# Seven half-block products in two more groups of layer one, and their input sums made at the end of attention

## The chip, the cores and the metric

The program runs on one core of one Trainium2 chip. The metric is device time in microseconds (us): the median of three runs. One further execution was taken by the hardware profiler, and its trace gives the rows below. Engines are named as the profile names them: PE (matmul), PEld (weight load), DVE (vector), ACT (scalar), POOL (GpSimd), SP (the queue that issues most DMAs).

## The reference, cut to what matters

```python
def _attn_ref(q, k, v):                      # 2 batches, 8 heads, 768 tokens, 64 wide
    k_sum = k.reshape(B, H, nb, block, D).max(axis=3)
    v_sum = v.reshape(B, H, nb, block, D).mean(axis=3)
    scores_l = scale * np.matmul(q, k.transpose(0, 1, 3, 2))      # kept where |i - j| < 16
    scores_s = scale * np.einsum('bhsd,bhnd->bhsn', q, k_sum) + np.log(block)
    ...                                      # softmax over both together
    return np.matmul(a, v_all)

def _moe_ref(x, w_in, w_out):                # 1536 tokens, 512 -> 2048 -> 512
    h = x @ w_in
    g = h * (1.0 / (1.0 + np.exp(-1.702 * h)))
    return g @ w_out

def _moe2_ref(x, w_gate, w_val, w_out):      # 512 -> 1536 (twice) -> 512
    gate = 1.0 / (1.0 + np.exp(-(x @ w_gate)))
    return gate * (x @ w_val) @ w_out
```

The attention's output is the input of layer one (`_moe_ref`), whose output is the input of layer two (`_moe2_ref`).

## The kernel before, in words

**Numbers in two parts.** Each operand of a layer's products is held as a high and a low half (`xH`/`xL`, `w..H`/`w..L`, `gh`/`gl`), and each product is three matmuls of 128x128 weights by 512 columns: high by low, low by high, high by high. A weight arrives as 64-bit words in `raw`. `load` turns it into the halves: DVE takes `da` (L125) and `db` (L128) from the words, ACT scales `da` (L126), DVE joins them (L132), ACT casts the high half (L135), DVE subtracts for the low half (L137).

**Tiles.** There are three blocks of 512 tokens (0, 1, 2). Layer one's hidden width of 2048 is cut into eight groups of 256 columns (`g` 0 to 7), layer two's 1536 into six. For each group and block, `first` makes two hidden tiles (24 matmuls, `ps_h`); ACT takes the sigmoid, DVE multiplies (`sg`, L399), ACT casts `gh` (L400), POOL subtracts for `gl` (L401). Then `second` multiplies by the group's rows of `w_out` (24 matmuls, four tiles `ps_o`), which DVE adds to `acc` (L464); of group 0, ACT copies them (L460).

**Paired groups.** From group `PAIRED` on, blocks 0 and 1 are not computed one by one: `pair` makes a 2x2 product of half blocks with seven products of six matmuls (`product`) in place of eight. For that it needs sums of quarters of the weight (`ws`, L151, then a cast and a subtraction into `s..H` and `s..L`, L158 and L160) and four sums of halves of the blocks 0 and 1 (`input_sums`: whole values `f1` to `f3`, split into `t1`, `t2`, `t3`, and a fourth that overwrites block 1's own tile). Block 2 goes through `single`.

**Order.** Attention has 24 units (batch, group of tokens, pair of heads). A loop over `t` issues each unit's steps with lags: scores `ps_s`, exponentials, the transposition `ps_p` (L633), its copy `pt` out of PSUM (L638, on DVE from unit 10 on), the product with v `ps_x` (L652), then the halves of x: ACT's cast `xH` (L670) and DVE's subtraction `xL` (L673). The `filler` issues layer one's groups 0 and 1 for blocks 0 and 1 in between. After attention come the `steps`: `first` of block 2 for groups 0 and 1, then groups 2 and 3 block by block, each step's `second` after the next step's `first`; then the paired groups. `pull` and `folding` issue pieces of weight loading and of the input sums between them. On top of that, a scheduler at build time chooses the order on each engine by what it expects of each instruction; DVE instructions marked `keep_in_program_order` keep their order among themselves. Each engine runs its own queue in order. The places for weights (`w_a` 8, `w_b` 6, of which `w_b` exists only after attention), the PSUM tiles and the tiles of `tp` are handed on when their last reader is done.

Of the kernel before, what the change touches and what calls it, by code (L numbers as in the profile page):

```python
# [9 lines left out]
F32 = mybir.dt.float32  # L10
F32R = mybir.dt.float32r
# [3 lines left out]
ALU = mybir.AluOpType  # L15
AX = mybir.AxisListType
PSUM = bass.MemoryType.PSUM
P = 128
# [11 lines left out]
def attention_moe_moe2_kernel(ctx: ExitStack, tc: tile.TileContext, ins: dict, out: bass.AP):  # L30
    nc = tc.nc
# [17 lines left out]
    TB = 512  # L49
# [55 lines left out]
    pool([sg_slots], 2, "sg_a")  # L105
    acc_a = ctx.enter_context(tc.tile_pool(name="acc_a", bufs=1))
    ps_h = ctx.enter_context(tc.tile_pool(name="ps_h", bufs=2, space=PSUM))

    def load(layer, g, i, early):

        while len(w_free) < 2:
            yield
        raw, shape = raws.pop(0)
        n = raw.shape[1] // 2
        words = raw.rearrange("p (n t) -> p n t", t=2)
        tail, head = words[:, :, 0], words[:, :, 1]
        a, b = (wtmp.tile([P, n], U32, tag=f"d{x}", name=f"d{x}") for x in "ab")
        af = a.bitcast(F32)  # L120
        ts = nc.vector.tensor_scalar
        hi, lo = (take(list(shape), f"w{layer}_{g}_{i}{x}", (layer, g, i)) for x in "HL")
        flat = "p a n -> p (a n)"

        ts(out=af, in0=head.bitcast(F32), scalar1=F64_MAX, scalar2=-F64_MAX, op0=ALU.min, op1=ALU.max)  # L125
        nc.scalar.activation(af, af, AF.Prelu, scale=REBIAS, alpha=-2.0 ** 32)  # L126
        yield
        ts(out=b, in0=tail, scalar1=29, scalar2=None, op0=ALU.logical_shift_right)  # L128
        if not early:
            fetch()  # L130
        yield
        nc.vector.scalar_tensor_tensor(  # L132
            out=a, in0=a, scalar=3, in1=b, op0=ALU.logical_shift_left, op1=ALU.bitwise_or
        )
        nc.scalar.copy(hi.rearrange(flat), af)  # L135
        yield
        nc.vector.tensor_tensor(out=lo.rearrange(flat), in0=af, in1=hi.rearrange(flat), op=ALU.subtract)  # L137
        weights[layer, g, i] = hi, lo
        yield
        if layer == 1 and (g < PAIRED or i == 1) or layer == 2 and i == 2:  # L140
            yield
            return
        w = af.rearrange("p (a n) -> p a n", n=shape[2])
        s = wtmp.tile([P, 4, KC // 2, P], F32, tag="db", name=f"ws{layer}_{g}_{i}")
        for n, x, y, op in (
            (0, block(w, 1, 0), block(w, 1, 1), ALU.add),
            (1, s[:, 0], block(w, 0, 0), ALU.subtract),
            (2, block(w, 0, 0), block(w, 1, 0), ALU.subtract),
            (3, block(w, 0, 1), s[:, 1], ALU.subtract),
        ):  # L150
            nc.vector.tensor_tensor(out=s[:, n], in0=x, in1=y, op=op)  # L151
            if n == 1:
                yield
        while len(w_free) < 2:
            yield
        sh, sl = (take([P, 4, KC // 2, P], f"s{layer}_{g}_{i}{x}", (layer, g, i, "s")) for x in "HL")
        flat = "p a k f -> p (a k f)"
        nc.scalar.copy(sh.rearrange(flat), s.rearrange(flat))  # L158
        yield
        nc.vector.tensor_tensor(out=sl.rearrange(flat), in0=s.rearrange(flat), in1=sh.rearrange(flat), op=ALU.subtract)  # L160
        weights[layer, g, i, "s"] = sh, sl
        yield
# [28 lines left out]

    mats = {1: [w_in, w_out], 2: [w_gate, w_val, w_out2]}
    pieces, weights, raws = [], {}, []
    PAIRED = 4
    wanted = [(1, g, i) for g in range(n1) for i in range(2)] + [(2, 0, 0), (2, 0, 1)]
    for g in range(n2):
        wanted += [(2, g + 1, 0)] * (g + 1 < n2) + [(2, g, 2)] + [(2, g + 1, 1)] * (g + 1 < n2)
# [20 lines left out]
        return t[:, (LO, HI)[j], i * P:(i + 1) * P]  # L218

    def t_tile(name):  # L220
        return tp.tile([P, KC // 2, TB], F32R, tag=f"t{name}", name=f"t{name}")

    def input_sums():

        def tt(**x):
            tc.keep_in_program_order(nc.vector.tensor_tensor(**x))

        f1, f2, f3 = (tp.tile([P, KC // 2, TB], F32, name=f"f{n}") for n in "123")  # L230
        h1, l1, h3, l3 = (t_tile(x) for x in ("1H", "1L", "3H", "3L"))

        def whole(to, blk, half):
            tt(out=to, in0=xH[blk][:, half], in1=xL[blk][:, half], op=ALU.add)

        whole(f1, 0, LO)
        yield
        whole(f3, 1, LO)
        yield
        tt(out=f1, in0=f3, in1=f1, op=ALU.subtract)  # L240
        yield
        whole(f2, 1, HI)
        yield
        tt(out=f3, in0=f2, in1=f3, op=ALU.subtract)
        nc.scalar.copy(h3, f3)
        yield
        tt(out=f2, in0=f2, in1=f1, op=ALU.subtract)
        nc.scalar.copy(h1, f1)
        yield
        nc.gpsimd.tensor_tensor(out=l3, in0=f3, in1=h3, op=ALU.subtract)  # L250
        yield
        nc.gpsimd.tensor_tensor(out=l1, in0=f1, in1=h1, op=ALU.subtract)
        yield
        h2, l2 = t_tile("2H"), t_tile("2L")
        h4, l4 = xH[1][:, LO], xL[1][:, LO]
        whole(f3, 0, HI)
        yield
        tt(out=f3, in0=f3, in1=f2, op=ALU.subtract)
        nc.scalar.copy(h4, f3)
        nc.scalar.copy(h2, f2)  # L260
        yield
        nc.gpsimd.tensor_tensor(out=l4, in0=f3, in1=h4, op=ALU.subtract)
        yield
        nc.gpsimd.tensor_tensor(out=l2, in0=f2, in1=h2, op=ALU.subtract)
        tsum.update({"1": (h1, l1), "2": (h2, l2), "3": (h3, l3), "4": (h4, l4)})
        yield

    def token_sums():

# [226 lines left out]
    with tc.manual_schedule(engines={mybir.EngineType.SP}), ExitStack() as es:  # L496
# [236 lines left out]
        def filler():  # L733
            for layer, g, blk in steps[:EARLY]:
                while (blk + 1) * 2 * HP - 1 + LD > now[0]:
                    yield
                need((1, g, 0))
                yield from first(layer, g, blk, batch=True)
                need((1, g, 1))
                yield from second(layer, g, blk, False, True)  # L740

        now = [0]
        fill = filler()
        for t in range(-1, NU + LD):
            now[0] = t

# [34 lines left out]
                pull(1 if t < 6 or t > 9 else 2)  # L781
            for _ in range(2 if t >= 8 else 1):
                next(fill, None)
        for _ in fill:
            pull(2)

    with tc.manual_schedule(engines={mybir.EngineType.SP}):
# [7 lines left out]
            for x, n in (("a", 4), ("b", 2))  # L795
        )
        ps_f, ps_s = Slots("h", (ps_a, 4)), Slots("h", (ps_h, 2), (ps_b, 2))
        folding, sums_1 = iter(()), input_sums()

        def run(main, rest=iter(()), after=()):  # L800

# [15 lines left out]
        for step in steps:  # L817
            need((*step[:2], 0))
            run(first(*step))
            if step[2] == 2:  # L820
                drop(*step[:2], 0)
            if prev:
                need((*prev[:2], 1))
                run(second(*prev, False))
                if prev[2] == 2:
                    drop(*prev[:2], 1)
            if step == (1, 2, 0):
                folding = itertools.islice(sums_1, 8)
            elif step == (1, PAIRED - 1, 1):
                for _ in folding:  # L830
                    pass
                folding = sums_1
            prev = step
        top = n1 - 1
        for g in range(PAIRED, n1):
# [94 lines left out]
```

## Time and profile before

| | before |
|---|---|
| three runs | 622.29, 622.41, 623.23 us; median 622.41 us |
| profiled execution | 623.11 us, its span 621.3 us |
| PE busy | 605.5 us, 97% of the span, 3138 instructions |
| DVE busy | 446.5 us, 72% |
| ACT busy | 297.0 us, 48% |
| POOL busy | 207.7 us, 33% |
| granted clock of PE | 1.00 throughout |

The span is the time from the first to the last instruction that the profile shows; the execution is 1.8 us longer. "Busy" of PE counts overlapping matmuls once, so a share of 97% says that PE had something under way, not that it ran at its peak.

### The profile page before, as it was taken

How to read it: one execution, taken by the hardware profiler on the slowest of the kernel's cores; microseconds unless marked ns; L12 is line 12 of the kernel's file. 1: busy time of each engine (PE TensorE's matmuls, PEld its weight loads, DVE VectorE, ACT ScalarE, POOL GpSimd, SP SyncE). 2: the span in 40 equal slices, each digit the busy share in tenths (PEclk: the TensorE clock that was granted, in tenths of full speed). 3: DMA queues.
4: the chain of work that ended last, by engine and by line, in shares of the span. 5: the costliest groups of instructions: out<-in, count | busy, mean ns of one | idle time of the engine just before them, and what ended most of it. 6: DMA issues, size and time to landing. Idle time of an engine off the chain costs nothing.

```text
span 621.3 us, 8331 instructions
## 1 busy us (share of the span) xinstructions
PE 605.5 (97%) x3138; PEld 493.4 (79%) x3138; DVE 446.5 (72%) x652; ACT 297.0 (48%) x580; POOL 207.7 (33%) x168
## 2 busy tenths in 40 slices
PE   7698999999999999999999999999999999999997
PEld 4576787788878888888888888888888888888886
DVE  6699666489998877887679996268488587493424
ACT  4688657565434353435346555454244353252210
POOL 6796685223453323223322031221220221120210
PEclk9999999999999999999999999999999999999999
DMA  9998743044121213031001214023024023000004
GB/s 307 339 311 295 233 134 70 0 137 136 68 69 68 69 24 112 25 112 64 5 18 51 68 69 136 1 69 129 7 68 136 0 74 131 0 2 0 1 34 170
DMA packets 25160, 58.08 MB, mean 93 GB/s; under 512 B 1568, under 2 KB 1824, under 8 KB 25120
## 3 DMA queue, kind: packets, MB, share of 16 engines
q1 hardware_dynamic: 24400, 56.24, 27.9%
q10 hardware_dynamic: 720, 1.31, 0.6%
q8 instruction: 25, 0.41, 0.3%
q14 instruction: 15, 0.12, 0.1%
HBM read 53.08 MB, written 3.15 MB: 90 GB/s over the span
## 4 chain that ended last, share of the span: by engine, by line
PE 81%; DMA 8%; DVE 5%; POOL 3%; issue 2%; ACT 1%; SPq 0%; POOLq 0%; ACTq 0%
PE ps_o L384 33%; PE ps_v L173 12%; PE ps_y L173 11%; PE ps_h L173 9%; PE ps_x L173 7%; PE ps_h L384 5%; DMA xH<-in_moe_w_out 3%; DMA k<-in_k 3%; DMA vt<-in_vt 2%; PE ps_s L600 2%; POOL gl L401 1%; PE ps_x L652 1%; PE ps_p L633 1%; DVE da L132 1%; DVE w_0L L137 1%
## 5 line engine op out<-in xcount | busy, mean ns | idle before, releaser
L401 POOL TENSOR_TENSOR gl<-sg,gh 128x512 fp32r<-128x512 f32 x84 | 121.9, 1455 | 364.6 <-ACT gh L400 309.6
L464 DVE TENSOR_TENSOR acc<-ps_o,acc 128x512 f32<-128x512 f32 x143 | 96.0, 684 | 56.7 <-PE ps_o L384 56.7
L400 ACT CAST gh<-sg 128x512 fp32r<-128x512 f32 x84 | 51.7, 620 | 67.7 <-DVE sg L399 47.3
L384 PE MATMUL ps_o<-gl,w_1H 128*128 128x512 f32 x192 | 75.5, 394 | 0.7 <-POOL gl L401 0.7
L384 PE MATMUL ps_o<-gh,w_1H 128*128 128x512 f32 x192 | 74.7, 390 | 0.0
L384 PE MATMUL ps_o<-gh,w_1L 128*128 128x512 f32 x192 | 72.1, 396 | 1.5 <-ACT gh L400 1.4
L384 PE MATMUL ps_o<-w_2H,gh 128*128 128x512 f32 (+1 forms) x146 | 56.4, 386 | 0.0
L384 PE MATMUL ps_o<-w_2L,gh 128*128 128x512 f32 (+1 forms) x146 | 56.4, 386 | 0.0
L384 PE MATMUL ps_o<-w_2H,gl 128*128 128x512 f32 (+1 forms) x146 | 55.9, 387 | 0.1
L132 DVE SCALAR_TENSOR_TENSOR da<-da,db 128x1024 uint32<-128x1024 uint32 x34 | 45.4, 1334 | 8.2 <-ACT da L126 7.6
L126 ACT ACTIVATE da<-da 128x1024 f32<-128x1024 f32 x34 | 36.0, 1060 | 19.9 <-DVE da L125 17.5
L384 PEld LDWEIGHTS ps_o<-gh,w_1L 128*128 128x128 f32 x192 | 35.9, 188 | 9.4 <-ACT gh L400 2.0
L384 PEld LDWEIGHTS ps_o<-gl,w_1H 128*128 128x128 f32 x192 | 36.1, 188 | 8.9 <-POOL gl L401 1.9
L384 PEld LDWEIGHTS ps_o<-gh,w_1H 128*128 128x128 f32 x192 | 36.1, 188 | 7.2
L589 POOL TENSOR_SCALAR kx<-k 128x384 f32<-128x384 f32 x24 | 32.4, 1351 | 20.2 <-DMA k<-in_k 11.2
L613 ACT ACTIVATE e<-ps_s,nm 128x128 f32<-128x128 f32 x96 | 34.3, 381 | 9.3 <-DVE nm L605 8.2
L384 PE MATMUL ps_h<-xL,w_0H 128*128 128x512 f32 x96 | 37.6, 392 | 0.4 <-DVE xL L673 0.4
L384 PE MATMUL ps_h<-xH,w_0L 128*128 128x512 f32 x96 | 37.7, 401 | 0.0
L384 PE MATMUL ps_h<-xH,w_0H 128*128 128x512 f32 x96 | 37.4, 390 | 0.0
L384 PEld LDWEIGHTS ps_o<-w_2H,gl 128*128 128x128 f32 x146 | 27.4, 188 | 6.1 <-DVE acc L464 0.3
L399 DVE TENSOR_TENSOR sg<-ps_h,sg 128x512 f32<-128x512 f32 x32 | 21.8, 684 | 14.3 <-ACT sg L408 12.2
L384 PEld LDWEIGHTS ps_o<-w_2H,gh 128*128 128x128 f32 x146 | 27.4, 188 | 5.6
(223 smaller groups left out, 1410.1 us busy)
## 6 DMA issues: line engine op xcount, KB each, us to landing
raw<-in_moe_w_out SPq DMA_DIRECT2D x13, 1024.0 KB, 4.9
raw<-in_moe_w_in SPq DMA_DIRECT2D x8, 1024.0 KB, 7.5
raw<-in_moe_w_gate SPq DMA_DIRECT2D x6, 1024.0 KB, 5.0
raw<-in_moe_w_val SPq DMA_DIRECT2D x6, 1024.0 KB, 5.1
q<-in_q SPq DMA_DIRECT2D x20, 256.0 KB, 9.5
vwin<-in_v SPq DMA_DIRECT2D x6, 768.0 KB, 9.7
k<-in_k SPq DMA_DIRECT2D x8, 400.0 KB, 7.6
out<-acc SPq DMA_DIRECT2D x11, 256.0 KB, 2.0
```

What stands on the lines that cost most here:

```text
L126: nc.scalar.activation(af, af, AF.Prelu, scale=REBIAS, alpha=-2.0 ** 32)
L132: nc.vector.scalar_tensor_tensor(out=a, in0=a, scalar=3, in1=b, op0=ALU.logical_shift_left, op1=ALU.bitwise_or)
L137: nc.vector.tensor_tensor(out=lo.rearrange(flat), in0=af, in1=hi.rearrange(flat), op=ALU.subtract)
L173: nc.tensor.matmul(ps, lhsT=a[x][:, kk, :], rhs=b[y][:, kk, :], start=start and i == 0, stop=i == n - 1, skip_group_check=True,)
L384: nc.tensor.matmul(ps, lhsT=a, rhs=b, start=i == 0, stop=i == n - 1)
L399: nc.vector.tensor_tensor(out=sg, in0=val, in1=sg, op=ALU.mult)
L400: nc.scalar.copy(gh, sg)
L401: nc.gpsimd.tensor_tensor(out=gl, in0=sg, in1=gh, op=ALU.subtract)
L464: nc.vector.tensor_tensor(out=a[:, m, :], in0=ps, in1=a[:, m, :], op=ALU.add)
L589: nc.gpsimd.tensor_scalar(out=to, in0=x, scalar1=scale, scalar2=None, op0=ALU.mult)
L600: nc.tensor.matmul(ps[:, j, :], lhsT=t[:, j, :], rhs=kt[:, j, :], start=False, stop=j == G - 1)
L613: nc.scalar.activation(e[:, j, :], s[:, j, :], AF.Exp, bias=nm[:, j:j + 1], accum_out=sm[:, j:j + 1])
```

## The change

`PAIRED` goes from 4 to 2: groups 2 and 3 of layer one go through `pair` and `single` too. Their weights get sums as well. The input sums are therefore wanted much sooner. Six sums of halves and the split of `t1` are issued one piece per iteration of the attention loop once t is over 18, the rest after attention, beside layer one's first steps; `f1` to `f3` and `t1` get memory of their own that exists during attention. The low halves of `t1` and of the fourth sum are made by DVE, those of `t2` and `t3` by POOL as before.

```diff
+    fp, t1p = (ctx.enter_context(tc.tile_pool(name=n, bufs=1)) for n in ("fp", "t1p"))
...
-    PAIRED = 4
+    PAIRED = 2
...
+        def split(name, f, slow):
+            if name == "4":
+                h, l = xH[1][:, LO], xL[1][:, LO]
+            else:
+                p = t1p if name == "1" else tp
+                h, l = (p.tile([P, KC // 2, TB], F32R, tag=f"t{name}{x}", name=f"t{name}{x}") for x in "HL")
+            nc.scalar.copy(h, f)
+            yield
+            if slow:
+                nc.gpsimd.tensor_tensor(out=l, in0=f, in1=h, op=ALU.subtract)
+            else:
+                tt(out=l, in0=f, in1=h, op=ALU.subtract)
+            tsum[name] = h, l
+            yield
...
         tt(out=f3, in0=f2, in1=f3, op=ALU.subtract)
-        nc.scalar.copy(h3, f3)
         yield
         tt(out=f2, in0=f2, in1=f1, op=ALU.subtract)
-        nc.scalar.copy(h1, f1)
-        yield
-        nc.gpsimd.tensor_tensor(out=l3, in0=f3, in1=h3, op=ALU.subtract)
-        yield
-        nc.gpsimd.tensor_tensor(out=l1, in0=f1, in1=h1, op=ALU.subtract)
...
+        yield from split("1", f1, False)
+        yield "rest"
+        yield from split("2", f2, True)
+        whole(f1, 0, HI)
+        yield from split("3", f3, True)
+        tt(out=f1, in0=f1, in1=f2, op=ALU.subtract)
+        yield from split("4", f1, False)
...
-        fill = filler()
+        fill, sums_1 = filler(), input_sums()
+        early = iter(lambda: next(sums_1), "rest")
         for t in range(-1, NU + LD):
...
+            if t > 4 * HP - 1 + LD:
+                next(early, None)
+        for _ in early:
+            pass
         for _ in fill:
             pull(2)
...
-        folding, sums_1 = iter(()), input_sums()
+        folding = sums_1
...
-            if step == (1, 2, 0):
-                folding = itertools.islice(sums_1, 8)
-            elif step == (1, PAIRED - 1, 1):
-                for _ in folding:
-                    pass
-                folding = sums_1
```

What this does to the order on the engines is seen at three places. Line numbers of the changed kernel are one to four higher: L642 is the copy `pt`, L677 is `xL`, L468 the addition to `acc`, L403 the multiplication `sg`, L405 the subtraction `gl`, L656 `ps_x`, L637 `ps_p`; L232 is every DVE instruction of the input sums, L243 POOL's.

**DVE, the last units of attention.** Before, from the multiplication of the last hidden tile of block 1, group 1, through the last three units into the first weight of group 2:

```order
L399 TENSOR_TENSOR sg_1564<-ps_h_1531,sg_1564 128x512
L673 TENSOR_TENSOR xL2_1246<-ps_x_1506,xH2_1245 128x256
L638 COPY pt_1549<-ps_p_1544 128x512
L673 TENSOR_TENSOR xL2_1246<-ps_x_1551,xH2_1245 128x256
L638 COPY pt_1581<-ps_p_1576 128x512
L464 TENSOR_TENSOR acc1_1_1425<-ps_o_1594,acc1_1_1425 128x512
L464 TENSOR_TENSOR acc1_1_1425<-ps_o_1602,acc1_1_1425 128x512
L673 TENSOR_TENSOR xL2_1246<-ps_x_1583,xH2_1245 128x256
L137 TENSOR_TENSOR w1_2_0L_1681<-da_1678,w1_2_0H_1680 128x1024
L464 TENSOR_TENSOR acc1_1_1425<-ps_o_1610,acc1_1_1425 128x512
```

Now, from the same multiplication on:

```order
L403 TENSOR_TENSOR sg_1582<-ps_h_1545,sg_1582 128x512
L232 TENSOR_TENSOR t1L_1560<-f1_1271,t1H_1559 128x1024
L677 TENSOR_TENSOR xL2_1252<-ps_x_1474,xH2_1251 128x256
L232 TENSOR_TENSOR f3_1273<-f2_1272,f3_1273 128x1024
L642 COPY pt_1518<-ps_p_1513 128x512
L468 TENSOR_TENSOR acc1_1_1437<-ps_o_1613,acc1_1_1437 128x512
L468 TENSOR_TENSOR acc1_1_1437<-ps_o_1621,acc1_1_1437 128x512
L677 TENSOR_TENSOR xL2_1252<-ps_x_1520,xH2_1251 128x256
L232 TENSOR_TENSOR f2_1272<-f2_1272,f1_1271 128x1024
L642 COPY pt_1567<-ps_p_1562 128x512
L468 TENSOR_TENSOR acc1_1_1437<-ps_o_1629,acc1_1_1437 128x512
L232 TENSOR_TENSOR f1_1271<-xH0_327,xL0_328 128x1024
```

```order
L468 TENSOR_TENSOR acc1_1_1437<-ps_o_1637,acc1_1_1437 128x512
L677 TENSOR_TENSOR xL2_1252<-ps_x_1569,xH2_1251 128x256
L642 COPY pt_1600<-ps_p_1595 128x512
L677 TENSOR_TENSOR xL2_1252<-ps_x_1602,xH2_1251 128x256
L138 TENSOR_TENSOR w1_2_0L_1700<-da_1697,w1_2_0H_1699 128x1024
L152 TENSOR_TENSOR ws1_2_0_1787<-da_1697 128x256
L152 TENSOR_TENSOR ws1_2_0_1787<-ws1_2_0_1787,da_1697 128x256
L232 TENSOR_TENSOR f1_1271<-f1_1271,f2_1272 128x1024
L152 TENSOR_TENSOR ws1_2_0_1787<-da_1697 128x256
L152 TENSOR_TENSOR ws1_2_0_1787<-da_1697,ws1_2_0_1787 128x256
L126 TENSOR_SCALAR da_1823<-raw1_2_1_921 128x1024
L232 TENSOR_TENSOR xL1_772<-f1_1271,xH1_771 128x1024
```

Four instructions of the input sums (and `f3`, `f1` and `f2` as whole values, further up) stand between the copies and subtractions of the last units; after the last unit come the weight's sums and two more input sums, followed by `s1_2_0L` and only then the first `sg` of block 2.

**PE, the last units of attention.** The tiles `ps_o` are group 1's second product for block 1, `ps_h` the first product of group 0 for block 2. Before:

```order
L652 MATMUL ps_x_1551<-pt_1549,vwin_109 64x64 x8
L633 MATMUL ps_p_1576<-ident_67,e_1472 128x128 x4
L384 MATMUL ps_o_1594<-gl1_1_1_1_1572,w1_1_1H_849 128x512
L384 MATMUL ps_o_1594<-gh1_1_1_1_1571,w1_1_1H_849 128x512
L384 MATMUL ps_o_1602<-gl1_1_1_1_1572,w1_1_1H_849 128x512
L384 MATMUL ps_o_1602<-gh1_1_1_1_1571,w1_1_1H_849 128x512
L652 MATMUL ps_x_1583<-pt_1581,vwin_109 64x64 x8
L384 MATMUL ps_o_1610<-gh1_1_1_0_1566,w1_1_1L_850 128x512
```

Now:

```order
L388 MATMUL ps_o_1637<-gh1_1_1_1_1589,w1_1_1L_856 128x512
L388 MATMUL ps_o_1637<-gl1_1_1_1_1590,w1_1_1H_855 128x512
L388 MATMUL ps_o_1637<-gh1_1_1_1_1589,w1_1_1H_855 128x512
L656 MATMUL ps_x_1569<-pt_1567,vwin_115 64x64 x8
L637 MATMUL ps_p_1595<-ident_67,e_1485 128x128 x4
L656 MATMUL ps_x_1602<-pt_1600,vwin_115 64x64 x8
L388 MATMUL ps_h_1677<-xH2_1251,w1_0_0L_259 128x512
```

The last unit's product now follows its own transposition directly; the twelve matmuls of `ps_o` that stood behind it stand ahead of the last two units. One unit more (`ps_x_1474` and a transposition) has moved behind the hidden tiles of block 1, group 1. In what stands between these rows, eight matmuls of `ps_o` (ending with two by `gh1_1_1_1`) now run without a break up to the first by `gl1_1_1_1`.

**POOL, the first gates after attention.** Now:

```order
L405 TENSOR_TENSOR gl1_1_1_1_1590<-sg_1582,gh1_1_1_1_1589 128x512
L243 TENSOR_TENSOR t2L_1704<-f2_1272,t2H_1703 128x1024
L243 TENSOR_TENSOR t3L_1754<-f3_1273,t3H_1753 128x1024
L405 TENSOR_TENSOR gl1_0_2_0_1693<-sg_1690,gh1_0_2_0_1692 128x512
L405 TENSOR_TENSOR gl1_0_2_1_1722<-sg_1719,gh1_0_2_1_1721 128x512
L405 TENSOR_TENSOR gl1_1_2_0_1746<-sg_1743,gh1_1_2_0_1745 128x512
```

Before, the two `L243` rows are not there: `gl` of group 0's block 2 follows `gl` of group 1's block 1, and POOL made its subtractions for the sums much later, among the gates of group 2.

## Rows read from the trace of the kernel before

**Rows 1.** Busy time by engine in three stretches: PE, PEld, DVE, ACT, POOL, clock, DMA.
```profile
100.00:127.00 27.00, 26.96 (x226) 20.94 (x225) 14.47 (x31) 16.45 (x51) 10.74 (x10) 1.00 0.01 2
127.00:160.00 33.00, 33.00 (x148) 27.31 (x147) 29.37 (x37) 19.67 (x27) 9.08 (x6) 1.00 0.40 128
160.00:210.00 50.00, 49.54 (x217) 40.39 (x216) 44.98 (x51) 20.70 (x29) 26.26 (x14) 1.00 0.19 64
```

**Rows 2.** PE's waits over the whole span, one releaser: total, times, longest.
```profile
PE ps_o L384 <- POOL gl L401: 0.7, 2, 0.4
```

**Rows 3.** PE in order of time: start, duration; 24 plain matmuls lie from first to second.
```profile
154.09 0.39 PE L384 MATMUL ps_h<-xH,w_0L 128*128 128x512 f32 x1
...
159.53 0.39 PE L384 MATMUL ps_o<-gh,w_1L 128*128 128x512 f32 x1
...
183.12 0.51 PE L384 MATMUL ps_o<-gl,w_1H 128*128 128x512 f32 x1 [0.45 <-POOL gl L401]
```

**Rows 4.** DVE in order of time, 155 to 167 us.
```profile
155.10 0.41 DVE L151 TENSOR_TENSOR ws<-ws,da 128x256 f32<-128x256 f32 x1
...
162.74 1.21 DVE L228 TENSOR_TENSOR f<-f,f 128x1024 f32<-128x1024 f32 x1
...
164.48 0.68 DVE L464 TENSOR_TENSOR acc<-ps_o,acc 128x512 f32<-128x512 f32 x1
165.07 1.21 DVE L132 SCALAR_TENSOR_TENSOR da<-da,db 128x1024 uint32<-128x1024 uint32 x1
166.21 0.68 DVE L464 TENSOR_TENSOR acc<-ps_o,acc 128x512 f32<-128x512 f32 x1
166.81 2.82 DVE L228 TENSOR_TENSOR f<-f,f 128x1024 f32<-128x1024 f32 x1
```

**Rows 5.** POOL in order of time: subtractions of the input sums, and a gate.
```profile
165.12 3.43 POOL L252 TENSOR_TENSOR t1L<-f,t1H 128x1024 fp32r<-128x1024 f32 x1 [2.85 <-ACT t1H L248]
168.51 2.28 POOL L401 TENSOR_TENSOR gl<-sg,gh 128x512 fp32r<-128x512 f32 x1
...
176.98 2.41 POOL L264 TENSOR_TENSOR t2L<-f,t2H 128x1024 fp32r<-128x1024 f32 x1 [3.39 <-ACT t2H L260]
```

**Rows 6.** POOL in order of time, 52 to 56 us.
```profile
52.56 1.04 POOL L627 TENSOR_TENSOR e<-e,rr 128x512 f32<-128x512 f32 x1
53.56 2.14 POOL L589 TENSOR_SCALAR kx<-k 128x384 f32<-128x384 f32 x1
```

**Rows 7.** DVE in order of time: one weight load, and three places around attention's end.
```profile
52.98 1.70 DVE L132 SCALAR_TENSOR_TENSOR da<-da,db 128x1024 uint32<-128x1024 uint32 x1
...
118.89 0.69 DVE L399 TENSOR_TENSOR sg<-ps_h,sg 128x512 f32<-128x512 f32 x1 [2.03 <-ACT sg L408]
...
130.50 0.69 DVE L399 TENSOR_TENSOR sg<-ps_h,sg 128x512 f32<-128x512 f32 x1
...
139.31 0.69 DVE L399 TENSOR_TENSOR sg<-ps_h,sg 128x512 f32<-128x512 f32 x1
```

**Rows 8.** PE in order of time, from the third last unit to the end of attention.
```profile
118.16 0.69 PE L652 MATMUL ps_x<-pt,vwin 128*64 128x64 f32 x16
118.77 0.66 PE L633 MATMUL ps_p<-ident,e 128*128 128x128 f32 x4
119.19 0.47 PE L384 MATMUL ps_o<-gh,w_1L 128*128 128x512 f32 x1
...
126.89 0.39 PE L384 MATMUL ps_h<-xH,w_0L 128*128 128x512 f32 x1
```

**Rows 9.** POOL in order of time: the last gate of attention.
```profile
120.32 1.29 POOL L401 TENSOR_TENSOR gl<-sg,gh 128x512 fp32r<-128x512 f32 x1 [1.44 <-ACT gh L400]
```

**Rows 10.** ACT in order of time: a cast of the same gate, of 1024 columns, a copy.
```profile
119.62 0.62 ACT L400 CAST gh<-sg 128x512 fp32r<-128x512 f32 x1 [0.36 <-DVE sg L399]
...
124.57 1.05 ACT L135 CAST w_0H<-da 128x1024 fp32r<-128x1024 f32 x1
...
140.92 0.59 ACT L460 COPY acc<-ps_o 128x512 f32<-128x512 f32 x1 [0.21 <-PE ps_o L384]
```

More of the change, by code (lines that the diff above doesn't have):

```diff
@@ L150, in load @@
         ):
-            nc.vector.tensor_tensor(out=s[:, n], in0=x, in1=y, op=op)
+            ins = nc.vector.tensor_tensor(out=s[:, n], in0=x, in1=y, op=op)
+            if (layer, g) == (1, PAIRED):
+                tc.keep_in_program_order(ins)
             if n == 1:
@@ L220, in t_tile @@
     def t_tile(name):
-        return tp.tile([P, KC // 2, TB], F32R, tag=f"t{name}", name=f"t{name}")
+        p = t1p if name[0] == "1" else tp
+        return p.tile([P, KC // 2, TB], F32R, tag=f"t{name}", name=f"t{name}")
     def input_sums():
@@ L228, in tt @@
             tc.keep_in_program_order(nc.vector.tensor_tensor(**x))
-        f1, f2, f3 = (tp.tile([P, KC // 2, TB], F32, name=f"f{n}") for n in "123")
-        h1, l1, h3, l3 = (t_tile(x) for x in ("1H", "1L", "3H", "3L"))
+        def split(name, f, slow):
[12 more added lines that the diff above has]
+            yield
         def whole(to, blk, half):
             tt(out=to, in0=xH[blk][:, half], in1=xL[blk][:, half], op=ALU.add)
+        f1, f2, f3 = (fp.tile([P, KC // 2, TB], F32, tag=f"f{n}", name=f"f{n}") for n in "123")
         whole(f1, 0, LO)
@@ L244, in input_sums @@
         tt(out=f3, in0=f2, in1=f3, op=ALU.subtract)
-        nc.scalar.copy(h3, f3)
         yield
         tt(out=f2, in0=f2, in1=f1, op=ALU.subtract)
-        nc.scalar.copy(h1, f1)
-        yield
-        nc.gpsimd.tensor_tensor(out=l3, in0=f3, in1=h3, op=ALU.subtract)
-        yield
-        nc.gpsimd.tensor_tensor(out=l1, in0=f1, in1=h1, op=ALU.subtract)
[L253 to L266, printed above, removed]
+        yield from split("1", f1, False)
[5 more added lines that the diff above has]
+        yield from split("4", f1, False)
     def token_sums():
```

## The prediction

> **What bounds the kernel now.** I read three views in this order: the page's busy times, the table by stretch, and the orders in time of the stretch that the change touches. PE is the bound nearly everywhere. Between 100 and 210 us it has something under way for 109.5 of 110 us [rows 1], and over the whole span it waits for POOL's gates, the commonest late input of the two layers, for 0.7 us in all [rows 2]. A matmul of 512 columns takes its turn every 0.227 us: 24 of them from 154.09 to 159.53 us [rows 3]. So a matmul less is worth 0.227 us, and a stall of PE is lost whole.
>
> The second thing to see is how near DVE is. It has work for 14.5 of 27 us at attention's end, but for 29.4 of 33 us just after, and 45.0 of 50 us after that [rows 1]: little is left there for a queue that starts late. Its prices: 1.14 us until the next start for a sum of 1024 columns (L132 at 165.07, next start 166.21; L228 has the same duration of 1.21), 0.6 us for a 512-column operation on PSUM (164.48 to 165.07), 0.41 us for a weight quarter [rows 4]. These hold only while POOL is idle. At 166.81 the same L228 took 2.82 us, because POOL's `t1L` was under way until 168.55; POOL's next gate took 2.28 us instead of 1.29 because that L228 ran until 169.63 [rows 4, 5, 9]. Yet `acc`, which reads PSUM, took its usual 0.68 us in the middle of `t1L` [rows 4]. So operations between SBUF tiles exclude each other on DVE and POOL. Who had waited went first: `kx` could follow at 53.56, but L132, waiting since 52.98, ended at 54.68, and `kx` took 2.14 us [rows 6, 7].
>
> The Trainium skill says this too (SBUF — State Buffer, section "Who interferes with whom"): a DVE operation with two SBUF inputs and a POOL operation that reads SBUF lock each other out for a whole instruction, and one with an input in PSUM does not take part; the trace agrees, with 2.82 us for the one and 0.68 us for the other.
>
> **The change, part by part.** *Fewer matmuls.* Each of two groups makes 7 x 6 = 42 matmuls for blocks 0 and 1 instead of 2 x 24 = 48. 12 x 0.227 = **-2.7 us**.
>
> *More work beside PE.* Per group DVE gets four weight quarters, a split and two additions of half products, 4 x 0.41 + 1.2 + 2 x 0.7 = 4.2 us; ACT three copies and a cast, about 2.8 us. ACT (19.7 of 33 us) hides that; DVE has 3.6 us free there [rows 1], but the input sums, eight instructions of 1.2 us, leave its queue later on. In total DVE can pay; what costs is when. No DMA is added, and SP's queue is unchanged.
>
> *A. The last units of attention.* I walk the new order with these prices, clock 0 at the issue of `ps_x_1474`, the place that stands at 118.16 in the trace. A `ps_x` takes 0.61 us of PE, a `ps_p` 0.42 [rows 8]. The second `sg` starts at 0.73 as now (118.89 [rows 7]), its gate's cast ends at 2.08 (120.24 [rows 10]), and POOL could start `gl` at 2.16. But `t1L` on DVE holds the tiles' port from 1.33 to 2.47, so `gl` ends at 3.76. PE reaches it after `ps_x`, `ps_p` and eight matmuls at 2.92: **0.9 us** idle. DVE wants `f3` from 2.81 on, gets it after `gl`, ends it at 4.90 and the copy `pt_1518` at 5.58; PE, four matmuls on, has waited since 4.71: **0.9 us**. Then twelve matmuls hide the next sum. After `pt_1567`, DVE has an addition, `f1`, an addition and `xL` ahead of `pt_1600` (0.6 + 1.14 + 0.6 + 0.34), which ends at 12.14. PE finished the last transposition at 10.48 and has nothing in between: **1.7 us**. The first matmul of block 2 comes at 12.8. Now it comes at 126.89 - 118.16 = 8.7 us [rows 8], to which the unit that moved adds 1.03: 9.8. That is +3.0 us. Ahead of this, `f3` and `f1` stand before two other units' copies; half a sum each, 2 x 0.5 us (bounds 0 and 2). **A = +4.0 us**, bounds 0.8 (only the last wait, less what stands there now) and 6.
>
> *B. The first gates of block 2.* Clock 0 at the first matmul of block 2. `t2H` and `t3H` are cast before `xH` of the last unit and `w1_2_0H`, a cast of 1.05 us [rows 10], so that weight is ready at 1.4. By then POOL has gone from `t2L` into `t3L`, 2.41 us each [rows 5], and holds until 3.5. DVE then does `w1_2_0L`, four quarters, two input sums, a `da` and `s1_2_0L`: 1.14 + 4 x 0.41 + 2 x 1.14 + 0.6 + 1.14 = 6.8 us. The first `sg` starts at 10.3; now it starts at 130.50 - 126.89 = 3.6 [rows 7, 8]. The fourth `sg` (block 2 of group 1) follows 8.8 us behind the first now (139.31 [rows 7]); from 10.3 that gives 19.1 (18.0 if the shorter list between them pays only today's waits; 19.6 if each of three SBUF operations meets a gate). Its cast, and the copy of the first `acc` tile that stands behind it on ACT, 0.6 us each [rows 10], free PE's fifth `ps_o` tile at 21.2. PE wants it after 48 + 24 + 6 matmuls, 78 x 0.227 = 17.7. **B = +3.5 us**, bounds 0 and 4.
>
> *C. Group 2's gates.* DVE stays behind while it loads group 3. The nearest row is the wait of 0.45 us for a late gate at 183.12 [rows 3]; three more gates (block 1 twice, block 0) stand as tight: 3 x 0.45 = **+1.3 us**, bounds 0 and 3. Further on the order is today's, and DVE has the time of the sums that left.
>
> Sum: -2.7 + 4.0 + 3.5 + 1.3 = **+6.1 us**. On the profiled execution that is a span of 621.3 + 6.1 = 627.4 and a time of 629.2 us; it lies 0.7 above the median of the runs, 622.41, so I predict 622.41 + 6.1 = **628.5 us**.
>
> **The rivals.** *Full gain:* every chain above is hidden, as 97% of PE suggests; 622.4 - 2.7 = 619.7 us, which is the other side. It decides if DVE's sums fall into its idle half of 100 to 127 us without touching a copy, which the last `pt_1600` contradicts: nothing is left to hide it. The Trainium skill's rule (Perfetto Trace Analysis, "Identifying the Most-Contended Engine") would have it so, since it has one improve the engine with the highest occupancy, here PE; the sum would then be its first term alone, and no run so far tests that.
>
> *Gain and loss cancel:* DVE and POOL meet less often than I walk. Without meetings, A's first two waits fall to 0.5 and 0.3 and the third stays, about 2.2 net of today; B vanishes, since `w1_2_0L` starts 2.1 us sooner and the three operations wait for no gate, and C with it: 622.4 - 2.7 + 2.2 + 0.5 = 622.4 us.
>
> *Worse:* POOL keeps the port from one instruction to the next, or ACT's queue adds its own order. Then each of some four DVE sums waits a gate more (1.1 us): +10.5, 633 us. The 2.14 us of `kx` [rows 6] speak against it, but C's bound of 3 leads there too.
>
> **How the numbers follow.** Chances: forecast (625 to 631.5) 0.62, worse 0.20, cancelled 0.12, full gain 0.06. The range 622.5 to 633.5 leaves out the full gain, half of the cancelled case and the worst third of the worse one, 0.06 + 0.06 + 0.07. 0.2%, 1.2 us, is about what a measurement of this kernel can tell from no change. Faster by more: 0.06; within: 0.11; slower by more: 0.83.
>
> **What would show it.** Right: 12 matmuls fewer; PE waiting for `pt` by DVE before the last `ps_x`, about 1.7 us; the first matmul of block 2 at about 130 to 131 us; a wait of some 3 us of PE before the fifth `ps_o` after attention, released by ACT; `w1_2_0L` taking over 2 us or starting late behind `t2L` and `t3L`; from 215 us on, PE without waits. Wrong: if the last copy is not held up, A fails; if the first gate of block 2 is cast within 6 us of the first matmul, B fails, and the time is below 625.

## The result, and the profile after

Predicted were 628.5 us with a range of 622.5 to 633.5. The changed kernel takes **627.95 us** (median of 4 runs, 627.64 to 628.58), the one before, on the same chip, 622.82 (4 runs, 622.29 to 623.40): a ratio of 1.0078, 95% interval 1.0066 to 1.009. It is slower by 5.1 us. The profiled execution has a span of 626.8 us against 621.3; PE runs 3126 matmuls instead of 3138, DVE is busy for 457.4 us instead of 446.5.

The same three stretches as in [rows 1], a little shifted because attention ends later:

```profile
core 0: us, PE busy (x) PEld busy (x) DVE busy (x) ACT busy (x) POOL busy (x), PEclk, DMA share, GB/s
100.00:131.00 31.00, 28.51 (x235) 22.25 (x234) 23.43 (x40) 19.51 (x55) 13.76 (x11) 1.00 0.01 2
131.00:165.00 34.00, 30.98 (x125) 23.94 (x124) 32.62 (x38) 18.99 (x28) 10.92 (x6) 0.95 0.30 95
165.00:215.00 50.00, 50.00 (x222) 41.42 (x221) 43.61 (x57) 24.99 (x39) 18.38 (x12) 1.00 0.25 83
```

PE, which had 109.5 of 110 us filled here, now lacks 2.5 us at attention's end and 3.0 us behind it. From 165 us on it is full again. The waits of PE, first from 95 to 131 us, then from 131 us on (in us: total, times, longest), say for whom:

```profile
PE ps_x L656 <- DVE pt L642: 1.8, 2, 1.4
PE ps_o L388 <- POOL gl L405: 0.6, 1, 0.6
...
PE ps_o L388 <- ACT acc L464: 2.2, 1, 2.2
PE ps_o L388 <- POOL gl L405: 0.8, 2, 0.6
```

Before, the trace has no such wait in the first stretch and 0.4 us in the second.

**Attention's end.** The order in time on DVE (start, duration, idle time before and its releaser in brackets) has the input sums (L232) ahead of the copies `pt` (L642):

```profile
118.81 1.22 DVE L232 TENSOR_TENSOR t1L<-f,t1H 128x1024 fp32r<-128x1024 f32 x1
...
120.28 1.97 DVE L232 TENSOR_TENSOR f<-f,f 128x1024 f32<-128x1024 f32 x1
122.17 0.68 DVE L642 COPY pt<-ps_p 128x512 f32<-128x512 f32 x1
...
126.71 1.22 DVE L232 TENSOR_TENSOR f<-xH,xL 128x1024 f32<-128x1024 f32 x1
127.84 0.69 DVE L468 TENSOR_TENSOR acc<-ps_o,acc 128x512 f32<-128x512 f32 x1
128.44 0.42 DVE L677 TENSOR_TENSOR xL<-ps_x,xH 128x256 fp32r<-128x256 f32 x1
128.77 0.68 DVE L642 COPY pt<-ps_p 128x512 f32<-128x512 f32 x1
```

The last copy ends at 129.45. PE, in its order in time, has waited 1.38 us for it, and starts block 2 at 130.13 instead of 126.89:

```profile
129.51 0.69 PE L656 MATMUL ps_x<-pt,vwin 128*64 128x64 f32 x16 [1.38 <-DVE pt L642]
```

**Block 2's first gates.** In the same order DVE, a little later:

```profile
131.60 1.23 DVE L138 TENSOR_TENSOR w_0L<-da,w_0H 128x1024 fp32r<-128x1024 f32 x1 [0.52 <-ACT w_0H L136]
132.74 2.62 DVE L152 TENSOR_TENSOR ws<-da 128x256 f32<-128x256 f32 x1
...
137.66 0.69 DVE L126 TENSOR_SCALAR da<-raw 128x1024 f32<-128x1024 f32 x1
138.27 1.22 DVE L232 TENSOR_TENSOR xL<-f,xH 128x1024 fp32r<-128x1024 f32 x1
139.41 1.22 DVE L163 TENSOR_TENSOR s_0L<-ws,s_0H 128x1024 fp32r<-128x1024 f32 x1
140.54 0.68 DVE L403 TENSOR_TENSOR sg<-ps_h,sg 128x512 f32<-128x512 f32 x1
```

And POOL, in its order in time:

```profile
129.34 2.40 POOL L243 TENSOR_TENSOR t2L<-f,t2H 128x1024 fp32r<-128x1024 f32 x1 [8.17 <-ACT t2H L240]
131.70 3.38 POOL L243 TENSOR_TENSOR t3L<-f,t3H 128x1024 fp32r<-128x1024 f32 x1
```

`w_0L` went ahead of `t3L` and kept it waiting; the weight quarter behind it then waited for `t3L`, 2.62 us instead of 0.41 [rows 4]. The first `sg` starts 10.4 us after block 2's first matmul (3.6 before). What this does to PE, in its own order:

```profile
149.07 0.39 PE L176 MATMUL ps_x<-xH,w_0H 128*128 128x512 f32 x1
151.66 0.50 PE L388 MATMUL ps_o<-gh,w_1L 128*128 128x512 f32 x1 [2.20 <-ACT acc L464]
...
153.43 0.61 PE L388 MATMUL ps_o<-gh,w_1H 128*128 128x512 f32 x1
153.84 0.63 PE L388 MATMUL ps_o<-gh,w_1L 128*128 128x512 f32 x1
```

The fifth `ps_o` waits 2.20 us for a copy of `acc` by ACT. And then something that was not predicted: from 153.43 on matmuls start 0.43 us apart instead of 0.227. The table by 2 us shows why in its clock column (1.00 is 2.4 GHz, 0.50 is 1.2):

```profile
150.00:152.00 2.00, 0.34 (x1) 0.30 (x2) 1.38 (x3) 1.70 (x4) 0.80 (x1) 1.00 0.65 106
152.00:154.00 2.00, 1.77 (x7) 1.12 (x6) 1.98 (x3) 1.93 (x3) 1.03 (x1) 0.86 1.01 393
154.00:156.00 2.00, 2.00 (x7) 1.52 (x6) 1.95 (x3) 1.52 (x3) 0.00 (x0) 0.50 0.07 25
156.00:158.00 2.00, 2.00 (x9) 1.61 (x8) 2.00 (x4) 1.48 (x3) 0.00 (x0) 0.79 0.00 0
```

PE was busy for 0.34 of 2 us, and the granted clock fell behind it. Eight matmuls, from 153.43 to 156.82, took 3.39 us where 8 x 0.227 = 1.8 do at full clock: 1.6 us. A busy share of 2.00 in 154 to 156 hides this; the count of 7 matmuls and the clock show it. This is the profiled execution, whose mean granted clock is 0.992; the other three have 0.994 to 0.997, and no trace shows whether each of them has this fall.

**The account**, by places that both traces have: 0.7 us before 69 us of the run, in a part whose order did not change (the first product with `w1_1_0` starts at 69.81, not 69.09; in the runs below that point scatters from 67.70 to 69.56; the clock reads 0.82 and 0.75 from 28 to 36 us and 0.73 and 0.84 from 56 to 64 us in this trace, and 1.00 in the trace before); +2.5 at attention's end; then, from block 2's first matmul to the first with `w1_5_0`, 104.0 us instead of 101.7, +2.3, which is -2.7 of matmuls, 0.59 + 2.20 + 0.23 = 3.0 of waits, 1.6 of clock and 0.4 not placed. Behind that nothing. Sum +5.5.

### The profile page after: what moved, and what is told of

It is laid out like the page before. It is cut to its first block, busy times and chain, and to the rows that moved or that the text cites. A ratio compares the mean times of both kernels' runs of the same rounds, so it can differ in the third digit from the quotient of the medians.

```text
span 626.8 us, 8321 instructions
## 1 busy us (share of the span) xinstructions
PE 607.4 (97%) x3126; PEld 494.9 (79%) x3126; DVE 457.4 (73%) x668; ACT 302.0 (48%) x588; POOL 205.2 (33%) x166
## 4 chain that ended last, share of the span: by engine, by line
PE 87%; DVE 5%; DMA 5%; ACT 1%; issue 1%; POOL 0%; ACTq 0%; DVEq 0%; SPq 0%
PE ps_o L388 35%; PE ps_v L176 13%; PE ps_y L176 12%; PE ps_h L176 10%; PE ps_x L176 8%; DMA q<-in_q 3%; PE ps_h L388 3%; PE ps_s L604 3%; PE ps_x L656 2%; DMA vwin<-in_v 1%; PE ps_p L637 1%; DVE f L232 1%; DVE ws L152 1%; PE ps_s L602 1%; DVE acc L468 0%
## 5 line engine op out<-in xcount | busy, mean ns | idle before, releaser
L405 POOL TENSOR_TENSOR gl<-sg,gh 128x512 fp32r<-128x512 f32 x84 | 124.6, 1490 | 369.0 <-ACT gh L404 314.5
L468 DVE TENSOR_TENSOR acc<-ps_o,acc 128x512 f32<-128x512 f32 x143 | 96.4, 686 | 60.3 <-PE ps_o L388 60.2
L133 DVE SCALAR_TENSOR_TENSOR da<-da,db 128x1024 uint32<-128x1024 uint32 x34 | 46.9, 1379 | 7.5 <-ACT da L127 6.4
L593 POOL TENSOR_SCALAR kx<-k 128x384 f32<-128x384 f32 x24 | 33.7, 1404 | 17.6 <-PE ps_s L604 9.4
L604 PE MATMUL ps_s<-kx,q 128*128 128x128 f32 x192 | 30.7, 311 | 3.1 <-DMA q<-in_q 2.0
L604 PEld LDWEIGHTS ps_s<-kx,q 128*128 128x128 f32 x192 | 28.1, 220 | 6.2 <-POOL kx L593 2.1
L388 PEld LDWEIGHTS ps_o<-w_2L,gh 128*128 128x128 f32 x146 | 27.4, 188 | 5.5
L631 POOL TENSOR_TENSOR e<-e,rr 128x512 f32<-128x512 f32 x24 | 26.3, 1098 | 9.3 <-DVE rr L626 9.3
```

Source lines behind the costliest of these rows:

```text
L133: nc.vector.scalar_tensor_tensor(out=a, in0=a, scalar=3, in1=b, op0=ALU.logical_shift_left, op1=ALU.bitwise_or)
L388: nc.tensor.matmul(ps, lhsT=a, rhs=b, start=i == 0, stop=i == n - 1)
L405: nc.gpsimd.tensor_tensor(out=gl, in0=sg, in1=gh, op=ALU.subtract)
L468: nc.vector.tensor_tensor(out=a[:, m, :], in0=ps, in1=a[:, m, :], op=ALU.add)
L593: nc.gpsimd.tensor_scalar(out=to, in0=x, scalar1=scale, scalar2=None, op0=ALU.mult)
L604: nc.tensor.matmul(ps[:, j, :], lhsT=t[:, j, :], rhs=kt[:, j, :], start=False, stop=j == G - 1)
```

## The experiments

My theory was: the loss is DVE's order at two places (**A** at attention's end, **B** at block 2's first gates), and B's stall also costs the clock. The rivals: the new pools shift something from the start ("memory"); the paired groups themselves cost more than their six matmuls save ("half products"). Ratios are to runs of the kernel before on the same chip, median 623.3 us throughout. The changed kernel's own reference was 622.82, so a difference between it and one of these runs is uncertain by some 0.5 us.

### Early sums alone, and memory alone

The first kernel is the changed one with `PAIRED = 4` again: sums at attention's end, groups 2 and 3 block by block.

```diff
-    PAIRED = 2
+    PAIRED = 4
...
-        folding = sums_1
+        folding = iter(())
...
+            if step == (1, PAIRED - 1, 1):
+                folding = sums_1
```

> Seven sums at attention's end as in the changed kernel, but groups 2 and 3 computed block by block as before (3138 matmuls). My theory (the order in DVE's queue costs, part A alone): PE waits for pt ahead of the last units, the first matmul of block 2 comes 2.5 to 3.3 us later than before (at about 129.5 to 130), nothing is lost between 130 and 165 us, and the time is before + 2.5 to + 3.5, about 625.7 us. Rival 'half products' (the loss comes from the paired groups themselves): the time of before, 622.8. Rival 'memory' (the two new pools shift things from the start on): before + 0.7, with the shift already there at 40 us.

The second is the kernel before with its tiles in the new pools:

```diff
+    fp, t1p = (ctx.enter_context(tc.tile_pool(name=n, bufs=1)) for n in ("fp", "t1p"))
...
-        f1, f2, f3 = (tp.tile([P, KC // 2, TB], F32, name=f"f{n}") for n in "123")
+        f1, f2, f3 = (fp.tile([P, KC // 2, TB], F32, tag=f"f{n}", name=f"f{n}") for n in "123")
```

> The kernel before with nothing but the memory moved: f1 to f3 and t1 in the two new pools, which exist during attention. My theory: no change, 622.8 within 0.5 us, and the granted clock in the first 70 us as before. Rival 'memory': 0.7 us more, there from 40 us on, as the changed kernel's first product with w1_0_0 came at 39.11 instead of 38.46 us.

Memory alone is worth nothing: 623.57 us, 1.0005 (0.9997 to 1.0014). Early sums alone cost 629.15 us, 1.0097 (1.0079 to 1.0114). A is there (block 2 starts at 129.10, after three waits of 0.62, 0.47 and 0.94 us), but 5.9 us is nearly three times these waits, and more than the whole change: the 625.7 us that I expected is missed by 3.4. The surplus lies further on. PE waits 1.25 us for a gate of POOL at 214.72, and, where neither edit reaches, at the end of layer one, 2.0 us for another, with its clock at 0.57 from 350 to 354 us.

The third of A's waits, 1.38 us in the changed kernel, says something more. In this run the sum `f1`, which stood ahead of the last copy there, is made later, and yet PE waits:

```profile
128.48 0.69 PE L656 MATMUL ps_x<-pt,vwin 128*64 128x64 f32 x16 [0.94 <-DVE pt L642]
```

So 0.94 of the 1.38 us are there without the sum and belong to the new order on PE, which has the last product right behind its own transposition; 0.44 are left for the sum.

### Late sums, with two and with one more paired group

The third kernel is the changed one with no sum inside attention:

```diff
-            if t > 4 * HP - 1 + LD:
-                next(early, None)
-        for _ in early:
-            pass
...
-        folding = sums_1
+        folding = iter(())
...
+            if step == (1, 0, 2):
+                folding = sums_1
```

> The seven products in groups 2 to 7 as in the changed kernel (3126 matmuls), but no input sum inside attention: all of them wait until the first step after attention is issued. My theory: part A is gone (first matmul of block 2 at 127 to 128), the first gate of block 2 is early again, so the stall of 2.2 us before the fifth ps_o and the clock's fall behind it go too; DVE's backlog then shows in groups 2 and 3 as several waits that sum to 2 to 4 us. Time 622 to 625, at least 3 us below the changed kernel. Rival 'half products': the waits of groups 2 and 3 take the whole loss, 627 or more.

The fourth has the seven products from group 3 on, and also late sums (as above, with the pieces up to t1 behind the first step and the others behind block 1 of group 2):

```diff
-    PAIRED = 2
+    PAIRED = 3
...
+            if step == (1, 0, 2):
+                folding = iter(lambda: next(sums_1), "rest")
+            if step == (1, PAIRED - 1, 1):
+                for _ in folding:
+                    pass
+                folding = sums_1
```

> The seven products from group 3 on (3132 matmuls, six fewer than before), the first seven input-sum pieces after attention, beside the steps of block 2 and group 2, the rest behind block 1 of group 2. My theory: neither A nor B; six matmuls give 1.4 us back and one or two waits of about 0.5 us in group 2 and 3 take part of it: 621 to 622.5, at or below before. Rival 'half products': each paired group costs more than its six matmuls, 623.5 or more.

Two groups: 625.18 us, 1.003 (1.0018 to 1.0042). A and B are gone as expected (block 2 at 127.24, clock 1.00), PE's order at attention's end is the old one again, and waits in groups 2 and 3 take their place, three for DVE and one for ACT, 4.1 us together:

```profile
PE ps_o L388 <- DVE acc L468: 1.3, 2, 0.8
PE ps_y L176 <- DVE sg L324: 1.2, 1, 1.2
PE ps_x L176 <- ACT ps_y L345: 1.1, 1, 1.1
PE ps_v L176 <- DVE t1L L232: 0.5, 1, 0.5
```

The time is 2.8 below the changed kernel, just short of the 3 that I expected, and 0.2 above the range. It is still 1.9 above the kernel before: with late sums, too, the two paired groups cost more than their twelve matmuls save.

One group: 627.19 us, 1.0059 (1.0039 to 1.0078). By its time this is the rival's number, 623.5 or more, and my theory had missed by 5 us. The trace says otherwise. Up to the last product with `w1_6_1` this run is 0.6 us ahead of before (333.85 against 334.45). The loss comes behind that. Its order on POOL:

```profile
338.30 7.86 POOL L405 TENSOR_TENSOR gl<-sg,gh 128x512 fp32r<-128x512 f32 x1 [10.55 <-ACT gh L404]
```

Meanwhile DVE, in the same columns:

```profile
338.09 1.21 DVE L282 TENSOR_TENSOR acc<-acc,acc 128x1024 f32<-128x1024 f32 x1
339.22 1.21 DVE L138 TENSOR_TENSOR w_0L<-da,w_0H 128x1024 fp32r<-128x1024 f32 x1
340.36 1.21 DVE L163 TENSOR_TENSOR s_0L<-ws,s_0H 128x1024 fp32r<-128x1024 f32 x1
341.49 1.21 DVE L289 TENSOR_TENSOR t2L<-acc,t2H 128x1024 fp32r<-128x1024 f32 x1
...
344.36 0.68 DVE L129 TENSOR_SCALAR db<-raw 128x1024 uint32<-128x1024 uint32 x1
```

A gate that takes 1.29 us [rows 9] takes 7.86. DVE has seven operations between SBUF tiles in a row, each of its usual length, each starting some 0.08 us before the one ahead of it ends; POOL gets in when they are over. PE waits for this gate 2.92 us, and the clock then reads 0.50 from 346 to 350 and 0.72 to 354:

```profile
346.22 0.80 PE L388 MATMUL ps_o<-gl,w_1H 128*128 128x512 f32 x1 [2.92 <-POOL gl L405]
```

Not every run of this kernel loses as much: three of the six took 625.37 to 626.0 us, with a mean granted clock of 0.997 to 1.000, and three 628.37 to 629.23, with 0.991 to 0.993. The trace is one of the latter. In the run with early sums the same gate took 7.81 us, from 341.52 on. So the theory needed a third place, **D**: POOL shut out by a DVE queue without gaps.

### The test of that: one gate on DVE

```diff
-        nc.gpsimd.tensor_tensor(out=gl, in0=sg, in1=gh, op=ALU.subtract)
+        (nc.vector if to == (1, 7, 2, 1) else nc.gpsimd).tensor_tensor(out=gl, in0=sg, in1=gh, op=ALU.subtract)
```

On top of the fourth kernel, and of the first:

> As the run with seven products from group 3 on and late sums (median 627.2 us), but one gate's low half, that of block 2's second hidden tile in group 7, is made by DVE instead of POOL. There POOL's subtraction took 7.86 us from 338.30 us on, while DVE ran seven operations between SBUF tiles back to back, and PE then waited 2.9 us and ran slowly for a while. Theory 'shut out' (POOL gets no turn while DVE's queue has such operations without a gap): DVE makes it in 0.7 us after three of them, the wait and the clock's fall go, and the time is 621.5 to 622.5, at or below before. Rival 'half products in group 3': they delay that place, and it stays at 626 or more. Rival 'late DVE': another gate is late in its place, 624 to 626.

> As the run with early sums and groups 2 and 3 block by block (median 629.2 us), with the same gate made by DVE. Theory: what is left is part A and two waits of 1.9 us behind it: the first matmul of block 2 at 129 to 130 us, no wait of PE between 335 and 360 us, and 626 to 627 us. Rival: the loss at the end of layer one has another cause and stays, 629.

Both came as expected, the first at the upper end of its range: **622.53 us, 0.9983 (0.9974 to 0.9993)**, and 626.88 us, 1.0062 (1.005 to 1.0075). In the first of them, the gate in DVE's order:

```profile
341.36 0.68 DVE L405 TENSOR_TENSOR gl<-sg,gh 128x512 fp32r<-128x512 f32 x1
```

And all that PE waits for from 95 us on:

```profile
PE ps_o L388 <- POOL gl L405: 0.4, 1, 0.4
PE ps_o L388 <- DVE acc L468: 0.2, 1, 0.2
```

By the medians the edit is worth 4.7 us in the one kernel and 2.3 in the other, both of which have D; the 4.7 holds the clock's fall of half of the runs. What is left of the early sums is A and the wait of 1.25 us at 214.88, +3.6 us with no matmul saved. The same edit in the kernel before, where D did not occur:

> The kernel before with nothing but the one gate of group 7 made by DVE instead of POOL. There that gate took 1.80 us and PE did not wait for it, so the edit should be worth nothing: 622.8 within 0.6 us. If it gains as much as the run with seven products from group 3 on and this gate, the gain there was the gate's and not that of the six matmuls saved.

622.75 us, 0.9995 (0.9986 to 1.0004): nothing that can be told. The first of these runs is the one version faster than both kernels, by 0.8 us of the 1.4 that six matmuls are worth. Its interval and this one's overlap, so that the gain is the matmuls' alone is likely by their count, not shown.

### B, taken apart

In the changed kernel, all low halves of the sums on DVE and the later pieces held back until the first step is issued; then the first half of that edit alone.

```diff
-        yield from split("2", f2, True)
+        yield from split("2", f2, False)
...
-        yield from split("3", f3, True)
+        yield from split("3", f3, False)
...
-        folding = sums_1
+        folding = iter(())
...
+            if step == (1, 0, 2):
+                folding = sums_1
```

> The changed kernel, with all low halves of the input sums on DVE (none on POOL) and the pieces after t1 held back until the first step after attention is issued. Theory (B: t2L and t3L on POOL ahead of the weight's low half and the first gate): A stays (block 2 from 130 us on), the first gate of block 2 is multiplied about 4 us after block 2's first matmul instead of 10.4, PE's wait behind group 0's product shrinks from 2.2 to 1 to 1.7 us, and with it the clock's fall: 624 to 626 us, 2 to 4 below the changed kernel. Rival 'weights' (the gate is late because DVE has group 2's weight to make, whoever does the sums): 627.5 or more.

> The changed kernel with one half of the last edit alone: t2L and t3L on DVE, 1.14 us each, in place of POOL's 2.4 and 3.4 us, and the pieces of the sums still issued right behind attention. Theory 'hold' (POOL's two subtractions shutting DVE out are what makes B): the first gate of block 2 comes about 6 us after block 2's first matmul, the wait behind it falls below 1.5 us, the clock stays at 1.00, and the time is 624 to 625. Rival 'amount' (what DVE has to do before the gates decides, whoever holds the port): DVE takes over 2.3 us and saves the 2.2 that its weight quarter waited; the third and fourth gate stay as late, PE waits 2 us or more, the clock falls as in the changed kernel: 626.5 to 628.

Together 624.21 us, 1.0009 (0.9997 to 1.0021); the first half alone (`split` without POOL) 624.44, 1.0015 (1.0006 to 1.0025). So moving POOL's two subtractions brings nearly all of it, 3.5 us, though DVE has 2.3 us more to do: "amount" does not hold. But the edit also changed the order on DVE. In the run with the first half alone the first `sg` stands ahead of three operations that it followed in the changed kernel:

```profile
135.37 0.69 DVE L403 TENSOR_TENSOR sg<-ps_h,sg 128x512 f32<-128x512 f32 x1
135.97 0.69 DVE L126 TENSOR_SCALAR da<-raw 128x1024 f32<-128x1024 f32 x1
136.57 1.22 DVE L232 TENSOR_TENSOR xL<-f,xH 128x1024 fp32r<-128x1024 f32 x1
137.71 2.32 DVE L163 TENSOR_TENSOR s_0L<-ws,s_0H 128x1024 fp32r<-128x1024 f32 x1
```

It comes 6.35 us after block 2's first matmul instead of 10.41. In the changed kernel the three took 2.88 us, from 137.66 to 140.54, so that most of these 4.1 us is the order. How much of the 3.5 us is POOL holding the port, and how much the order, is not separated by any run. Misses of detail: with both edits the first `sg` comes 6.3 us after block 2's first matmul, not 4; with the first alone the wait before `ps_o` is 1.72 us, not below 1.5. Here it is, in PE's order of the run with the first half alone:

```profile
148.72 0.50 PE L388 MATMUL ps_o<-gh,w_1L 128*128 128x512 f32 x1 [1.72 <-ACT acc L464]
```

The table by 2 us around it:

```profile
146.00:148.00 2.00, 1.00 (x5) 0.50 (x3) 1.04 (x1) 1.49 (x2) 1.76 (x2) 1.00 0.00 0
148.00:150.00 2.00, 1.28 (x6) 1.06 (x7) 1.74 (x3) 1.67 (x4) 0.17 (x1) 1.00 0.83 220
150.00:152.00 2.00, 2.00 (x10) 1.67 (x9) 1.97 (x4) 2.00 (x5) 0.00 (x0) 1.00 0.78 304
```

A wait 0.5 us shorter than that of the changed kernel, and the clock stays at 1.00: by the account above that alone would be 1.6 of the 3.5 us.

### The clock by itself

The kernel before, with the last unit's copy prolonged:

```diff
+            for _ in range(12 if u == NU - 1 else 0):
+                nc.vector.tensor_copy(t, t)
             live["pt", u] = t
```

> The kernel before, with the copy pt of the last unit of attention followed by 12 copies of that tile onto itself on DVE, so that PE has nothing to do for some us ahead of the last ps_x, about 125 us. Theory 'clock': after a stall of 2 us or more the granted clock falls from 1.00 to about 0.5 for 2 to 4 us, and the time grows by the stall and 1.5 to 2.5 us on top. Rival: the time grows by the stall alone and the clock stays at 1.00; then the fall at 154 us in the changed kernel had another reason.

The stall was longer than meant, as PE's order shows:

```profile
131.31 0.91 PE L654 MATMUL ps_x<-pt,vwin 128*64 128x64 f32 x12 [4.35 <-DVE pt L640]
```

The table by 2 us around it:

```profile
128.00:130.00 2.00, 0.00 (x0) 0.00 (x0) 1.83 (x6) 0.00 (x0) 0.00 (x0) 0.99 0.00 0
130.00:132.00 2.00, 0.69 (x12) 0.69 (x14) 1.19 (x3) 0.00 (x0) 0.00 (x0) 0.50 0.00 0
...
136.00:138.00 2.00, 2.00 (x9) 1.60 (x8) 0.89 (x1) 1.53 (x2) 0.00 (x0) 0.80 0.37 68
```

The clock falls while PE is idle, stays at 0.50 until 136 us and reads 0.80 from 136 to 138. The products of block 2 with `w1_0_0`, 5.2 us from the first to the last in the kernel before, take 7.4: 2.2 us for the clock. The whole run is 634.99 us, 1.0191 (1.0177 to 1.0205), 11.7 more; 5.5 of that is the later start of block 2 (the stall, and a wait of 0.6 us for `acc` ahead of it), 2.2 the clock, and 2.9 are three waits for `acc` by DVE between 181 and 195 us. About 1 us is not placed. So a fall of the clock follows a stall in this kernel without the change too; the total was outside what either theory gave, since neither had those waits.

## Why the prediction was right

**Fewer matmuls**: 12 fewer, -2.7, as counted.

**A** was right in its mechanism and too large in size: +2.5 instead of +4.0. All three waits that I walked are there, in the same order: 0.64 us for the gate (walked 0.9), 0.47 for `pt_1518` (0.9), 1.38 for the last copy (1.7), 2.5 together. The "half a sum each" for two earlier units, 2 x 0.5, did not occur. The run without sums in attention removes the waits, the run with early sums alone keeps 2.0 us of them. Not all of A is the sums in DVE's queue: 0.94 us of the last wait is there without a sum ahead of the copy, from the order on PE that came with them and that the walk had too ("has nothing in between").

**B** held in its times: first `sg` at 10.4 us (walked 10.3), the fourth at 19.3 (19.1), the copy of `acc` that frees the tile ended at 21.5 (21.2, of which the terms named there make 21.0). Its price came out lower, 2.2 instead of 3.5, since PE wanted the tile later, at 19.3 instead of 17.7: ahead of it stood 78 matmuls, as walked, but one of them had waited 0.59 us for a gate, and the others together took about 1 us longer than at 0.227 us each. With the 0.59 and 0.23 for gates B is 3.0 us. Of the cause that I named, POOL holding the port for `t2L` and `t3L`, the trace shows 2.2 us directly, in the quarter of 2.62 us; the run that takes them off POOL agrees, but it changed DVE's order as well, so that the port alone is not shown to be the cause.

**C** is the term that failed: no wait of PE from 165 us on, where I had +1.3. From one row of 0.45 us I had concluded on three more; DVE has 43.6 of 50 us to do there now, less than the 45.0 before [rows 1].

**What was missing** was the clock: +1.6 us, a term that the sum did not have. It made up for part of what A and C had too much, so that the sum, +6.1 predicted and +5.1 by the medians, is nearer than its parts are. That nearness is luck; the direction, and two of the three places, are not.

**The rivals.** *Full gain*: PE was lightened by 2.7 us and the kernel lost 5.1, since DVE, busy for 73% of the span, decides at two places when PE may go on. The Trainium skill's rule (Perfetto Trace Analysis, "Identifying the Most-Contended Engine") would have the engine with the highest occupancy lightened; for TensorE it wants the share of weight loading in place of that of matmuls. By either it is PE here (97% and PEld 79%, DVE 72%), and the full gain that the prediction drew from it did not come. *Gain and loss cancel*: it took B to vanish if DVE and POOL do not meet; taking two of the meetings away brought 624.4 us, 2.0 above its 622.4, in a kernel whose order on DVE had changed too, so that it stays untested as it stood. *Worse*: its mechanism, an engine that keeps the port from one instruction to the next, I had rejected by [rows 6], from which I read that who had waited goes first. That was a mistake of reasoning, although not of this forecast: it did not decide the changed kernel, but the engine that keeps it exists. It is DVE, not POOL, and at D it cost 2.3 to 4.7 us.

## What to carry to other kernels

Before moving work into an engine's spare time, read that time just where the work will stand: DVE had 12 us free at attention's end and still 2.5 us came onto PE's path, because sums stood ahead of copies for which PE waited, and because PE's own order no longer had anything to do before the last copy. Take POOL work with SBUF operands off a path that PE follows wherever DVE's queue is dense, since it may get no turn. And price a stall of PE with the slow matmuls that can follow it.

## What the runs showed of the hardware

**Who gets the port.** The Trainium skill (SBUF — State Buffer, "Who interferes with whom") calls the port pair that DVE and POOL share an exclusive lock, and says that issue order decides who blocks. The traces agree on the lock (a weight quarter of 0.41 us took 2.62 behind `t3L`), but not on the order: POOL's gate at 338.30 was issued ahead of DVE's at 339.22 and of five more, and went last. Where DVE's next operation began with a gap, a waiting POOL went in between (in the changed kernel, after a gap of 0.04 us, DVE's L129, at 144.38, took 1.66 us instead of 0.68 for a gate issued at 143.2). Where DVE's followed without a gap, it went either way: at 340.68 in the kernel before, DVE's `t3L` gave way to a gate and took 2.31 us. What decides there stays open.

**The clock.** With stalls of 2.00, 2.20, 2.92 and 4.35 us the granted clock fell to 0.50 (1.2 GHz) in these traces; with one of 1.72 us it stayed at 1.00 (2.4 GHz). It need not fall in every execution: of the kernel with the stall of 2.92 us one run has a mean granted clock of 1.000, at 625.37 us where the profiled one, at 0.991, took 628.44 (whether it had the stall too, no trace shows). At 0.50, matmuls of 512 columns start 0.427 us apart. The fall can come behind the stall, with matmuls already under way again at full speed (151.66 to 153.43 in the changed kernel).
